# Weight sums by accumulating transfers, one more block by seven products, and a new order for the second token group

## The chip, the cores and the metric

The kernel runs on one core of one Trainium2 chip. The metric is the device time of one execution in microseconds; the median of several executions is compared.

## The reference, cut to what matters

The program is a chunked state-space scan followed by a two-layer network with a sigmoid-weighted activation.

```
y = mamba2_ssd(x, a, B, C)            # 4 sequences, 8 heads, 768 steps, head size 32, state 16
h = y @ w_in                          # 3072 tokens x 256, w_in 256 x 2048
g = h * (1.0 / (1.0 + np.exp(-1.702 * h)))
out = g @ w_out                       # w_out 2048 x 256
```

The weights arrive as 64-bit floats and are rounded to 32 bits in the kernel.

## The kernel before, in words

The 3072 tokens are worked in six groups of 512 (`g` = 0 to 5), each of two pairs of chunks (`p`, `p + 1`). For each pair the scan part makes a decay table (`decay`, a VectorE scan into `L`, line 424, and two products into `Be`, line 489), scores (`score`, TensorE, line 682, masked inputs from `mask_blocks`, ScalarE, line 659), their weighting (`weigh`, VectorE, line 693), the state increments (`gain`, TensorE, line 713), the states (`keep_both`: ScalarE line 767 or VectorE line 769, then steps on VectorE, line 782), and the outputs (`finish`: `inter`, line 822, and `intra`, line 836, on TensorE, and copies into `yT` on ScalarE, lines 869 and 871). The scan part of group g + 1 is put between the products of group g.

The network has eight blocks `j` per group, each of 256 hidden units. There are two ways to work a block of the first layer. `hidden` (line 896) is the plain one: four matmuls of 128x128 by 512 columns for the block's two halves. `first` (lines 952 and 962) works the block as a 2x2 by 2x2 product with seven products of 256 columns instead of eight (Winograd's form). Its steps are named by digits: "1", "6", "7", "4" build up in one PSUM bank X and are copied out in between by ScalarE (line 957); "5", "2", "3" build up in a second bank Y. "D" adds (VectorE, line 1084), "S" and "T" activate (ScalarE, line 929). The second layer has the same two ways: `project_all` (line 994) plain, `product` (line 1057, in the last group line 1064) with seven products per block into one large PSUM area, combined at the group's end by `combine` (line 1088).

Seven products need sums of the weight quarters and of the data quarters. `mix_in(n)` makes four sums of `w_in` for blocks 2n and 2n + 1, `mix_w(n)` the same of `w_out`; each is four VectorE operations of 128x256 (lines 914 and 1017). `mix_y` and `mix_g` make the sums of the data, three VectorE operations each (lines 920 to 922). All weight sums are made once and used from group 1 on. Group 0 is plain throughout; in group 1 blocks 0 and 1 of the first layer are plain, all else is by seven products.

The order of work is written by hand: `in_order` keeps every engine in the order of the program text. During group 0's second layer, the table `in_project[0]` places other work ahead of a given `f`; `after` does so behind group 1's two pairs of plain calls; from then on a string such as "2.1 3.1 2.5" gives the order of steps, in which a digit pair is a block and its step, "P" is the next second-layer product, and a letter runs a given function. `steady(j)` and `closing(k)` are the repeated strings. VectorE, ScalarE and POOL work ahead of TensorE as far as their data allow.

Transfers are issued by SP's queue, in program order: tables `ra` (line 275), blocks of B and C (line 124), and `b`, `c`, `x` (line 150). `x` has three buffers: the `x` of a pair is loaded once the one three pairs earlier is read. POOL has little to do after 13 us: for each `clip_rows` a memset (line 511), a copy (line 513) and a small memset (line 514), which `decay_rows` (line 522) waits for.

SBUF tiles with one tag share a few buffers. `words` (tag "bits", four buffers of 2048 words a partition) holds the raw weights and later `ra` and the sums of `w_out`; "m" and "p2" (two each of 1024 words) hold parts of the raw weights and later the sums of `w_in`. In PSUM, the "ff" tag has four banks for X, Y, `hidden` and `gain`, and the "cb" area of four banks holds in turn the scores, the outputs of `finish` and the sums of the second layer.

Of the kernel before, what the change touches and what calls it, by code (L numbers as in the profile page):

```python
# [8 lines left out]
FP32 = mybir.dt.float32  # L9
# [6 lines left out]
GELU_SCALE = 1.702  # L16
# [19 lines left out]
def kernel(  # L36
# [224 lines left out]
    scratch = dram.tile([NC, 2, NB * NH, H], FP32, name="scratch")  # L261
    ra = {}

    def spread(p, held=False):

        if p - 2 in ra:
            ra[p] = ra[p - 2]
        else:
            ra[p] = words(f"a{p}").bitcast(FP32)[:, :2 * NH * H].rearrange(
                "p (k e) -> p k e", k=2)  # L270
        if held:
            nc.vector.memset(ra[p][:, 0, :1], 0.0)
        b, c = divmod(2 * p, NC)
        for i, side in enumerate(SIDES):
            nc.sync.dma_start(
                out=ra[p][side],
                in_=scratch[c:c + 2, i, b * NH:(b + 1) * NH].rearrange("c h i -> c (h i)").unsqueeze(
                    0).to_broadcast([H, 2, NH * H]))
# [625 lines left out]

    def mix_in(n):

        t = wide.tile([P, PN], FP32, tag=("m", "p2")[n % 2], name=f"mi{n}").rearrange(
            "p (j s e) -> p j s e", j=2, s=4)
        w = w_in[:, 4 * n:4 * (n + 1)].rearrange("p (j i) k e -> p j i k e", i=2)
        a11, a12, a21, a22 = w[:, :, 0, 0], w[:, :, 0, 1], w[:, :, 1, 0], w[:, :, 1, 1]  # L910
        s1, s2, s3, s4 = (t[:, :, i] for i in range(4))
        for o, u, v, op in ((s1, a21, a22, ALU.add), (s2, s1, a11, ALU.subtract),
                            (s3, a11, a21, ALU.subtract), (s4, a12, s2, ALU.subtract)):
            nc.vector.tensor_tensor(out=o, in0=u, in1=v, op=op)
        for k in range(2):
            mixed_in[2 * n + k] = t[:, k]

    def mix(t, B):

        nc.vector.tensor_tensor(out=t[:, 0:2], in0=B[:, :, 1], in1=B[:, 0], op=ALU.subtract)  # L920
        nc.vector.tensor_tensor(out=t[:, 2], in0=B[:, 1, 1], in1=t[:, 0], op=ALU.subtract)
        nc.vector.tensor_tensor(out=t[:, 3], in0=B[:, 1, 0], in1=t[:, 2], op=ALU.subtract)

# [3 lines left out]

    def silu(o, i):
        nc.scalar.activation(o, i, AF.Silu, scale=GELU_SCALE)  # L929

    def first(g, j, i):
# [4 lines left out]
        B = yT[g].rearrange("p k (t e) -> p k t e", t=2)  # L936
        T, S = mixed_y[g], mixed_in[j]
        A = w_in[:, 2 * j:2 * j + 2].rearrange("p i k e -> p k i e")
# [8 lines left out]
        if i in "1674":  # L947
            lhsT, rhs, copy = {"1": (A[:, 0, 0], B[:, 0, 0], s["ac"][:, 0]),
                               "6": (S[:, 1], T[:, 2], s["b"]),
                               "7": (S[:, 2], T[:, 1], s["ac"][:, 1]),  # L950
                               "4": (A[:, 1, 1], T[:, 3], None)}[i]
            nc.tensor.matmul(out=s["X"], lhsT=lhsT, rhs=rhs, start=i == "1", stop=i == "4",  # L952
                             skip_group_check=True)
            if copy is None:
                silu(gT[g, j][:, 1, :HT], s["X"])
            else:
                nc.scalar.activation(copy, s["X"], AF.Copy)  # L957
        elif i in "523":
            lhsT, rhs, o = {"5": (S[:, 0], T[:, 0], s["Y"][:, 1]),
                            "2": (A[:, 1, 0], B[:, 1, 0], s["Y"][:, 0]),  # L960
                            "3": (S[:, 3], B[:, 1, 1], s["Y"][:, 1])}[i]
            nc.tensor.matmul(out=o, lhsT=lhsT, rhs=rhs, start=s.pop("new", False), stop=i != "5",  # L962
                             skip_group_check=True)
            if i == "3":
                plus(gT[g, j][:, 0, HT:], s["Y"][:, 1], s["b"])
        elif i == "T":
            c12 = gT[g, j][:, 0, HT:]
            silu(c12, c12)
        else:
            if i == "D":  # L970
                block(g, j)
            c = gT[g, j].rearrange("p i (t e) -> p (i t) e", t=2)[:, 0:4:3]
            if i == "D":
                plus(c, s["Y"], s["ac"])
            else:
                silu(c, c)

# [9 lines left out]
    def project_all(g, between):  # L987

        o = [bank(f"o{g}_{c}") for c in range(2)]
        for f in range(NF):  # L990
            for do in between.get(f, []):
                do()
            for c in range(2):
                nc.tensor.matmul(out=o[c], lhsT=w_out[:, c, f],  # L994
                                 rhs=gT[g, f // 2][:, f % 2], start=(f == 0),
                                 stop=(f == NF - 1), skip_group_check=True)
        sums[g] = ffn.tile([P, 2, 2, HT], FP32, tag="gT", name=f"c{g}", bufs=6)
        for c in range(2):
# [6 lines left out]

    def mix_w(n):

        if n % 2 == 0:
            mixed_w["tile"] = words(f"mw{n}").bitcast(FP32).rearrange(
                "p (n j s e) -> p n j s e", n=2, j=2, s=4)  # L1010
        t = mixed_w["tile"][:, n % 2]
        w = w_out[:, :, 4 * n:4 * n + 4].rearrange("p c (j i) e -> p c j i e", i=2)
        a11, a12, a21, a22 = w[:, 0, :, 0], w[:, 0, :, 1], w[:, 1, :, 0], w[:, 1, :, 1]
        s1, s2, s3, s4 = (t[:, :, i] for i in range(4))
        for o, u, v, op in ((s1, a21, a22, ALU.add), (s2, s1, a11, ALU.subtract),
                            (s3, a11, a21, ALU.subtract), (s4, a12, s2, ALU.subtract)):
            nc.vector.tensor_tensor(out=o, in0=u, in1=v, op=op)
        for k in range(2):
            mixed_w[2 * n + k] = t[:, k]

# [7 lines left out]
    def product(g, j, only=ORDER, ks=range(2)):  # L1028
        if j == 0 and g not in acc:
# [3 lines left out]
            else:  # L1033
# [11 lines left out]

        terms = ((A[:, 0, 0], B[:, 0, 0]), (A[:, 0, 1], B[:, 1, 0]), (S[:, 1], T[:, 2]),
                 (S[:, 0], T[:, 0]), (S[:, 2], T[:, 1]), (S[:, 3], B[:, 1, 1]),
                 (A[:, 1, 1], T[:, 3]))
# [45 lines left out]
    def combine(g):  # L1094
# [5 lines left out]
        scaled(u[:, 1:3], a[:, 3:5], u[:, 2:3].to_broadcast([P, 2, HT]))  # L1100
        scaled(c[:, 1, 0], a[:, 6], u[:, 2])
        scaled(c[:, 0], a[:, 1:6:4], u[:, 0:2])
        sums[g] = c
        rest = lambda: plus(c[:, 1, 1], u[:, 2], u[:, 3])
        if g < NG - 2:
# [18 lines left out]
    def end(g, j0):  # L1124
# [21 lines left out]
        scaled(u2, p7, u2)  # L1146
        plus(c[:, 1, 1], u2, u5)
        put(1, nc.scalar)
        products(1)
        scaled(c[:, 1, 0], p4, u2)  # L1150
        scaled(c[:, 0, 0], p2, u1)
# [88 lines left out]
    for i, k, c in ((2, 1, 1), (3, 2, 3), (4, 4, 7), (5, 8, 10), (6, 10, 14), (7, 14, 15)):  # L1240
# [15 lines left out]
    at(in_project[0], 15, lambda: finish(pairs))  # L1256
    at(in_project[0], 13, lambda: mix_in(1), lambda: turn_blocks(2), lambda: decay(n))
    at(in_project[0], 6, lambda: spread(n), lambda: spread(n + 1), lambda: load_blocks(n),
# [6 lines left out]
    later = n, n + 1  # L1265
    at(after, "H0", lambda: decay(n + 1), lambda: mix_y(1), lambda: since_start(n),
       lambda: since_start(n + 1), lambda: gain(later), lambda: keep_both(later, True), lambda: score(later),
       lambda: weigh(n), lambda: weigh(n + 1))
    at(after, "H1", lambda: turn_out(0, 0), lambda: turn_out(0, 1), lambda: mix_in(2),
       lambda: mix_w(0))  # L1270
    assert [b for b in range(NB) if 3 * CG <= b * NC < 4 * CG] == [2]

# [5 lines left out]
    project_all(0, in_project[0])  # L1278
    mask_blocks(n)
    mask_blocks(n + 1)  # L1280
    load_blocks(p)
    spread_rows(2)
    load(p, "bx")
    for step in "H0", "H1":
        for i in range(2):
            hidden(1, 2 * int(step[1:]) + i)
        for do in after[step]:
            do()

# [37 lines left out]
    def more_loads():  # L1327
# [3 lines left out]

    run(1, "2.1 3.1 2.5 2.6 3.6 z 2.2 2.7 3.5 3.7 3.2 2.D 2.4 3.D 3.4 2.S W 3.S y m 2.3 3.3 4.1 2.T 3.T",
        m=lambda: mix_g(1, 0),
        z=lambda: finish(later, (0,)), y=lambda: finish(later, (1,)), W=lambda: clip_rows(2))
    mix_g(1, 1)
    more_loads()
    mix_in(3)
    decay_rows(2)
    run(1, "4.5 4.2 P P 4.6 P P 4.7 P P P 4.D", seven(1, 0))
    mix_w(1)  # L1340
    mix_g(1, 2)
    decay(p)
    between = {5: (lambda: mix_g(1, 3), lambda: mix_w(2)),
               6: (lambda: mix_g(1, 4), lambda: decay(p + 1)),
               7: (lambda: mix_g(1, 5), lambda: mix_w(3))}
    for j in range(5, NF // 2):
        run(1, steady(j), seven(1, j - 4), M=lambda: [do() for do in between[j]])
    k = NF // 2 - 1
    run(1, closing(k), seven(1, 4))
    mix_g(1, 6)  # L1350
    mix_in(0)
    run(1, "P P A P P P P P", seven(1, 5), A=lambda: ahead(2, p))
    mix_g(1, 7)

    for g in range(2, NG):
# [28 lines left out]
        def refill():  # L1384
            if most:
# [4 lines left out]
                spread(p + 1)  # L1390

        if more:

            run(g, "2.1 1.S 1.4 1.3 2.6 2.5 2.2 2.7 1.T 3.1 s 2.D 2.S w 2.4 2.3 3.6 M0 3.5 3.2 3.7 2.T 4.1 y "
                "refill 3.D 4.5 4.2 4.6 3.4 3.3 P P P 3.S P 3.T M1 4.7 P P P 4.D M2",
                seven(g, 0), s=lambda: score((n, n + 1)), w=lambda: (weigh(n), weigh(n + 1)),
                y=lambda: finish((n, n + 1)), refill=refill,
                M0=lambda: mix_g(g, 0), M1=lambda: mix_g(g, 1), M2=lambda: mix_g(g, 2))
# [61 lines left out]
```

## Time and profile before

| | |
|---|---|
| runs | 345.81, 345.05, 346.56 us; median 345.81 |
| the profiled execution | 345.17 us, of which its span 343.4 us |
| TensorE matmul busy | 338.3 us (98%) |
| VectorE busy | 255.5 us (74%), 486 instructions |
| ScalarE busy | 155.8 us (45%) |
| POOL busy | 13.3 us (4%), 40 instructions |
| transfers | 25.75 MB, mean 75 GB/s; SP's queue 34.8% of 16 engines' span |
| granted TensorE clock | 1.00 |

Group 0's first layer runs from 17.6 to 45.2 us, its second layer from 45.6 to 78.2, group 1 from there to about 131 us. Busy times of engines are not shares of the path: the chain of work that ended last says what set the end.

### The profile page before, as it was taken

What the parts mean: (1) busy time and instruction counts of PE and PEld (TensorE: products, weight loads), DVE (VectorE), ACT (ScalarE), POOL (GpSimd) and SP (SyncE); (2) the same over time, 40 slices, a digit from 0 to 9 for tenths busy, and PEclk for the clock granted to TensorE, in tenths of its full rate; (3) what the DMA queues carried; (4) which work ended last, traced back from release to release, by engine and by line L of the source; (5) the groups of instructions that cost most, each with busy time, mean ns of one, the idle gap of its engine ahead of it and who ended that gap; (6) DMA issues with size and microseconds to landing.
All of it is one profiled execution on the core that took longest, in us unless ns stands there. A gap on an engine that the chain in (4) does not pass through costs nothing.

```text
span 343.4 us, 8128 instructions
## 1 busy us (share of the span) xinstructions
PE 338.3 (98%) x3378; PEld 271.2 (79%) x3378; DVE 255.5 (74%) x486; ACT 155.8 (45%) x356; POOL 13.3 (4%) x40
## 2 busy tenths in 40 slices
PE   8999999999999999999999999999999999999996
PEld 6645744555788888888888888888888888899996
DVE  6989999999999797858995667787564653465463
ACT  5798672406563314554333554342553422554320
POOL 6100010200010000000000000000000000000000
DMA  6699978455737000345513036400000300000402
GB/s 166 138 296 210 323 158 151 107 84 106 116 80 123 7 2 22 56 111 92 108 32 46 2 86 115 63 3 0 2 3 2 61 2 0 0 2 0 63 0 62
DMA packets 90020, 25.75 MB, mean 75 GB/s; under 512 B 73440, under 2 KB 87264, under 8 KB 89984
## 3 DMA queue, kind: packets, MB, share of 16 engines
q1 hardware_dynamic: 89152, 24.72, 34.8%
q8 instruction: 26, 0.43, 0.6%
q10 hardware_dynamic: 832, 0.52, 0.5%
q14 instruction: 10, 0.08, 0.1%
HBM read 21.99 MB, written 3.24 MB: 73 GB/s over the span
## 4 chain that ended last, share of the span: by engine, by line
PE 97%; DMA 1%; ACT 0%; DVE 0%; issue 0%; ACTq 0%; DVEq 0%
PE acc L1057 28%; PE X L952 19%; PE Y L962 15%; PE h L896 10%; PE o L994 8%; PE acc L1064 7%; PE y L836 3%; PE cb L682 2%; PE y L822 1%; PE A L713 1%; PE ab L556 1%; DMA az<-in_a_dram 1%; PE tp L599 0%; DVE cum L359 0%; ACT yT L856 0%
## 5 line engine op out<-in xcount | busy, mean ns | idle before, releaser
L957 ACT ACTIVATE ac<-X 128x256 f32<-128x256 f32 x76 | 29.0, 382 | 83.9 <-PE X L952 83.8
L1057 PE MATMUL acc<-mg,mw 128*128 128x256 f32 x192 | 53.9, 379 | 0.0
L1084 DVE TENSOR_TENSOR gT<-Y,ac 128x512 f32<-128x512 f32 x38 | 26.2, 689 | 37.0 <-PE Y L962 34.5
L929 ACT ACTIVATE gT<-gT 128x512 f32<-128x512 f32 (+1 forms) x76 | 38.9, 519 | 26.1 <-DVE gT L1084 25.5
L952 PE MATMUL X<-my,mi 128*128 128x256 f32 x152 | 45.1, 379 | 0.0
L1057 PEld LDWEIGHTS acc<-mg,mw 128*128 128x128 f32 x192 | 36.5, 190 | 4.9
L1084 DVE TENSOR_TENSOR gT<-Y,b 128x256 f32<-128x256 f32 x38 | 16.0, 420 | 28.7 <-PE Y L962 28.7
L896 PE MATMUL h<-yT,w_in 128*128 128x512 f32 (+1 forms) x96 | 35.1, 524 | 0.5 <-ACT yT L856 0.5
L1057 PE MATMUL acc<-gT,w_out 128*128 128x256 f32 x128 | 35.5, 379 | 0.0
L952 PEld LDWEIGHTS X<-my,mi 128*128 128x128 f32 x152 | 28.2, 190 | 3.6
L896 PEld LDWEIGHTS h<-yT,w_in 128*128 128x128 f32 x96 | 18.1, 190 | 16.0 <-issue 12.4
L994 PE MATMUL o<-gT,w_out 128*128 128x512 f32 x64 | 28.3, 596 | 0.0
L920 DVE TENSOR_TENSOR mg<-gT 128x512 f32<-128x512 f32 x40 | 27.3, 681 | 0.0
L1057 PEld LDWEIGHTS acc<-gT,w_out 128*128 128x128 f32 x128 | 24.4, 190 | 3.3
L957 ACT ACTIVATE b<-X 128x256 f32<-128x256 f32 x38 | 14.6, 383 | 19.2 <-PE X L952 18.5
L962 PE MATMUL Y<-my,mi 128*128 128x256 f32 x76 | 23.0, 384 | 0.0
L952 PE MATMUL X<-my,w_in 128*128 128x256 f32 x76 | 22.8, 384 | 0.0
L962 PE MATMUL Y<-yT,w_in 128*128 128x256 f32 x76 | 22.7, 381 | 0.0
L962 PE MATMUL Y<-yT,mi 128*128 128x256 f32 x76 | 22.6, 381 | 0.0
L994 PEld LDWEIGHTS o<-gT,w_out 128*128 128x128 f32 x64 | 11.9, 190 | 13.6 <-issue 13.1
L952 PE MATMUL X<-yT,w_in 128*128 128x256 f32 x76 | 22.5, 379 | 0.0
L424 DVE TENSOR_TENSOR_SCAN L<-a,idents 128x1024 f32<-128x1024 f32 x9 | 20.5, 2279 | 0.0
(152 smaller groups left out, 546.2 us busy)
## 6 DMA issues: line engine op xcount, KB each, us to landing
a<-scratch SPq DMA_DIRECT2D x18, 256.0 KB, 4.6
bits<-in_moe_w_out_dram SPq DMA_DIRECT2D x8, 512.0 KB, 8.4
x<-in_x_dram SPq DMA_DIRECT2D x24, 128.0 KB, 3.7
out_dram<-ob SPq DMA_DIRECT2D x37, 64.0 KB, 2.0
bits<-in_moe_w_in_dram SPq DMA_DIRECT2D x8, 256.0 KB, 4.8
bits<-in_moe_w_in_dram SPq DMA_DIRECT2D x4, 512.0 KB, 8.9
b<-in_B_dram SPq DMA_DIRECT2D x20, 64.0 KB, 3.5
af<-in_a_dram SPq DMA_DIRECT2D x3, 384.0 KB
```

The lines of the kernel that those rows point to most:

```text
L424: nc.vector.tensor_tensor_scan(out=L, data0=ra[p].rearrange("p k e -> p (k e)"), data1=idents.rearrange("p h i -> p (h i)"), initial=0.0, ...
L836: nc.tensor.matmul(out=y[i][t][D * q:D * q + D, 2 * n + k], lhsT=rx[p][side, k, h], rhs=L[side, k, h // Q, h % Q], start=begin(i, t, (q,)) ...
L896: nc.tensor.matmul(out=h[:, cols], lhsT=w_in[:, f, k], rhs=yT[g][:, k, cols], start=(k == 0 and c == 0), stop=(k == NK - 1), skip_group_ch ...
L920: nc.vector.tensor_tensor(out=t[:, 0:2], in0=B[:, :, 1], in1=B[:, 0], op=ALU.subtract)
L929: nc.scalar.activation(o, i, AF.Silu, scale=GELU_SCALE)
L952: nc.tensor.matmul(out=s["X"], lhsT=lhsT, rhs=rhs, start=i == "1", stop=i == "4", skip_group_check=True)
L957: nc.scalar.activation(copy, s["X"], AF.Copy)
L962: nc.tensor.matmul(out=o, lhsT=lhsT, rhs=rhs, start=s.pop("new", False), stop=i != "5", skip_group_check=True)
L994: nc.tensor.matmul(out=o[c], lhsT=w_out[:, c, f], rhs=gT[g, f // 2][:, f % 2], start=(f == 0), stop=(f == NF - 1), skip_group_check=True)
L1057: nc.tensor.matmul(out=acc[g][0][i][:, cols], lhsT=w, rhs=h[:, cols], start=(j == 0 and k == 0 and (i, 0) in begins), stop=(j == NF // 2 - ...
L1064: nc.tensor.matmul(out=o[k] if type(o) is list else o[:, cols], lhsT=h[:, cols], rhs=w, start=(j == 0 and (i, k) in begins), stop=(j == NF ...
L1084: nc.vector.tensor_tensor(out=o, in0=v, in1=w, op=ALU.add)
```

## The change

Three things are changed together.

**Who makes the weight sums.** `sums_of` makes the four sums of a tile in four steps, by transfers that POOL's queue issues: step 0 copies one weight quarter into the first half and others into the second, step 1 adds the remaining weights to the first half, steps 2 and 3 add parts of the tile to each other. An added transfer has `accum_op=ALU.add`. Only additions are left, so signs go elsewhere: `mix` takes differences the other way round with `minus_both` (a scalar_tensor_tensor for a tensor_tensor), "4" and one half of "S" activate with the scale -1.702, so that "S" is two activations of 256 columns for one of 512, and the combination at the end of a group subtracts. `mix_in(2)`, `mix_in(3)` and all of `w_out`'s sums (now two calls of `mix_w`, each for four blocks) go this way, from group 0's second layer on. `mix_in(0)` and `mix_in(1)` stay on VectorE (`js=`), the first in two parts, one per block.

**Block 1 of group 1** goes by seven products for two plain `hidden` calls; block 0 stays plain.

**Group 1 in a new order.** `mix_in(1)`, `turn_blocks(2)` and `decay(n)` leave the table `in_project[0]` at 13, and with the rest of `after` they go into one string that begins with "M1 1.1 B h Q D4 K Y E i M0 A c s k". `decay_rows(2)` goes from ahead of block 4 into block 6's steady string. The two `turn_out(0, ...)` with their stores go to group 2; until then group 0's output lies in the unused half of a `ra` tile (`spare`).

```diff
-    ra = {}
+    ra, spare = {}, []
...
+            t = words(f"a{p}").bitcast(FP32)
+            ra[p] = t[:, :2 * NH * H].rearrange("p (k e) -> p k e", k=2)
+            spare.append(t[:, 2 * NH * H:])
...
+    SLOTS = {"3": (0, 0), "1": (0, 1), "2": (1, 0), "4": (1, 1)}
+
+    def sums_of(tiles, n, js, new, first, w, step):
+        if n not in tiles:
+            tiles[n] = new().rearrange("p (h j s e) -> p h j s e", h=2, j=js, s=2)
+        one, two = tiles[n][:, 0], tiles[n][:, 1]
+        def put(o, i, **how):
+            nc.gpsimd.dma_start(out=o, in_=i, **how)
+        if step == 0:
+            first(one)
+            put(two, w(0))
+        elif step == 1:
+            put(one, w(1), accum_op=ALU.add)
+        elif step == 2:
+            put(two[:, :, 0], one[:, :, 1], accum_op=ALU.add)
+        elif step == 3:
+            put(two[:, :, 1], two[:, :, 0], accum_op=ALU.add)
...
+    def mix_in(n, steps=range(4), js=None):
...
+        if js:
...
+            plus(one[:, :, 0], a[:, :, 0, 0], a[:, :, 1, 0])
+            plus(one[:, :, 1], a[:, :, 1, 0], a[:, :, 1, 1])
+            plus(two[:, :, 0], one[:, :, 1], a[:, :, 0, 0])
+            plus(two[:, :, 1], two[:, :, 0], a[:, :, 0, 1])
+            return
+        for step in steps:
...
+                lambda o: nc.gpsimd.dma_start(out=o.rearrange("p j s e -> p (j s) e"), in_=w[:, :, 0]),
...
     def mix(t, B):
-        nc.vector.tensor_tensor(out=t[:, 0:2], in0=B[:, :, 1], in1=B[:, 0], op=ALU.subtract)
-        nc.vector.tensor_tensor(out=t[:, 2], in0=B[:, 1, 1], in1=t[:, 0], op=ALU.subtract)
-        nc.vector.tensor_tensor(out=t[:, 3], in0=B[:, 1, 0], in1=t[:, 2], op=ALU.subtract)
+        nc.vector.tensor_tensor(
+            out=t[:, 0:2], in0=B.rearrange("p k t e -> p (k t) e")[:, 0:4:3],
+            in1=B[:, 0, 1:2].to_broadcast([P, 2, HT]), op=ALU.subtract)
+        minus_both(t[:, 2], t[:, 0], B[:, 1, 1])
+        minus_both(t[:, 3], t[:, 2], B[:, 1, 0])
...
-                silu(c, c)
+                for k in range(2):
+                    silu(c[:, k], c[:, k], 1 - 2 * k)
...
-        sums[g] = ffn.tile([P, 2, 2, HT], FP32, tag="gT", name=f"c{g}", bufs=6)
+        sums[g] = spare[-1].rearrange("p (c t e) -> p c t e", c=2, t=2)
...
-    at(in_project[0], 13, lambda: mix_in(1), lambda: turn_blocks(2), lambda: decay(n))
+    for k in range(4):
+        at(in_project[0], 7 + k, lambda k=k: mix_w(0, (k,)), lambda k=k: mix_in(2, (k,)))
+    for k in range(4):
+        at(in_project[0], 14, lambda k=k: mix_in(3, (k,)), lambda k=k: mix_w(1, (k,)))
...
-    run(1, "2.1 3.1 2.5 2.6 3.6 z 2.2 2.7 3.5 3.7 3.2 2.D 2.4 3.D 3.4 2.S W 3.S y m 2.3 3.3 4.1 2.T 3.T",
...
-    run(1, "4.5 4.2 P P 4.6 P P 4.7 P P P 4.D", seven(1, 0))
+    run(1, "M1 1.1 B h Q D4 K Y E i M0 A c s k 2.1 v 2.5 2.2 1.6 2.6 w 1.5 1.7 2.7 2.D 1.2 1.4 z 3.1 1.D 2.3 1.S 2.T G 1.3 2.S 3.6 3.2 y 3.7 C 4.1 3.5 3.D 2.4 1.T L P P H 4.6 P P P P 4.5 4.2 3.3 4.7 P 4.D 3.T I 3.S 3.4 N", seven(1, 0),
```

In the new string the letters stand for: M1 `mix_in(1)`, B `turn_blocks(2)`, h and i the two `hidden` calls of block 0, Q and K `mask_blocks` of the second and the first pair, D4 and E `decay` of the two pairs, Y `mix_y(1)`, M0 block 1's half of `mix_in(0)`, A `gain`, c `score`, s `since_start`, k `keep_both`, v and w `weigh` of the second and the first pair, z and y the two halves of `finish`, G, H and I `mix_g`, C `clip_rows(2)`, L loads for group 3, N `decay` for it.

## The prediction

> **What bounds the kernel now.** I read the page's first and fourth parts, then TensorE's own waits, then the table of engines by stretches of 10 us.
>
> ```profile
> PE 338.3 (98%) x3378; PEld 271.2 (79%) x3378; DVE 255.5 (74%) x486; ACT 155.8 (45%) x356; POOL 13.3 (4%) x40
> ...
> PE 97%; DMA 1%; ACT 0%; DVE 0%; issue 0%; ACTq 0%; DVEq 0%
> ```
>
> ```profile
> PE busy L468 <- DVE ones L313: 1.1, 1, 1.1
> PE h L896 <- ACT yT L856: 0.5, 1, 0.5
> PE ab L556 <- DVE cum L359: 0.3, 1, 0.3
> PE y L836 <- issue: 0.2, 1, 0.2
> PE b L629 <- ACT L L577: 0.2, 1, 0.2
> ```
>
> TensorE ends the chain and waits five times, 2.3 us in all, always before 17.58 us, which the change doesn't touch. Busy time of pipelined matmuls can hide gaps, so I also took the distances between matmul starts. From 17.58 to 340.7 us each record follows the last by its own width, 0.43 us for 512 columns and 0.216 for 256. The exceptions are 0.09 to 0.19 us where a run of small matmuls (lines 682, 713, 822, 836) begins or ends. So only less TensorE work can shorten the middle, and any new wait there lengthens the run one for one.
>
> ```profile
> 60.00:70.00 10.00, 10.00 (x139) 4.95 (x138) 9.61 (x15) 3.77 (x13) 2.56 (x3) 1.00 0.39 100
> 70.00:80.00 10.00, 10.00 (x203) 5.48 (x202) 9.93 (x12) 3.27 (x7) 0.00 (x0) 1.00 0.69 101
> 80.00:90.00 10.00, 10.00 (x195) 6.01 (x198) 9.16 (x22) 5.95 (x18) 0.00 (x0) 1.00 0.57 109
> 90.00:100.00 10.00, 10.00 (x196) 8.62 (x190) 9.42 (x23) 5.75 (x14) 0.66 (x2) 1.00 0.38 60
> ```
>
> Columns after the stretch: sum of time, then busy time of PE, PEld, DVE, ACT, POOL, then the granted clock (1.00), the DMA share and GB/s. Around the end of group 0 (78 us) VectorE has 9.2 to 9.9 us of work in 10: it is nearly late here, and here the order changes.
>
> **TensorE's part.** Each product shows as two records. Block 1 of group 1 costs two `hidden` calls now: eight records of 512 columns.
>
> ```profile
> 81.71 0.87 PE L713 MATMUL A<-x,Be 64*32 64x64 f32 x56
> 82.51 1.21 PE L682 MATMUL cb<-CT,Bt 32*64 32x128 f32 x64
> 83.65 3.70 PE L896 MATMUL h<-yT,w_in 128*128 128x512 f32 x8
> 87.19 1.03 PE L952 MATMUL X<-yT,w_in 128*128 128x256 f32 x4
> ```
>
> From 83.65 to 87.19 less one change of form (0.10) is 3.44 us. Seven products are 14 records of 0.216, 3.02 us. **Saved: 0.42 us.** Nothing else on TensorE changes in number.
>
> **VectorE's part.** Gone from group 1 are six calls of `mix_in`/`mix_w`, 24 additions of 128x256 at 0.42 us (lines 914, 1017): 10.1 us. Two transposes of line 1114 (1.3 us) go to group 2, where VectorE is 7.3 us busy in 10. `mix_in(0)` becomes eight additions of 128x128, at 0.28 each (row of line 769) 2.2 us for 1.7. `mix` swaps two tensor_tensor of 128x256 (425 ns) for scalar_tensor_tensor (424 ns, line 1088): nothing. None of this is on the path by itself, since TensorE waits for nothing.
>
> **ScalarE's part.** "S" becomes two activations of 128x256 (413 ns) for one of 128x512 (625): +0.2 us, 39 times, 7.8 us in all on an engine that is 45% busy. `mix_g`, which reads the result, stands about a block later in the steady order; before the last block's there is about 1 us to spare (first sum done at 332.5, wanted near 333.5). I cost it at nothing; without that cover it would be 0.2 us at that place.
>
> **The new start of group 1.** I put the operations in program order on three lines, with the durations above, from TensorE's 78.18 us. VectorE's order up to there is the same: four sums, two transposes, `decay(4)` to 78.0. Then `mix_y` comes first (1.5, to 79.6), `decay(5)` (2.7, to 82.3) and block 1's sums (1.1, to 83.4). TensorE does 1.1, h, i (0.43 + 1.72 + 1.72) to 82.05. `gain`, with its first half (0.5) on pair 4, wants pair 5 at about 82.5: just met, where 1 us was spare before. Two places are late:
>
> - "z" wants both `weigh` calls, because its area is theirs. VectorE reaches their end by 83.4 + 0.75 (`since_start`) + 2.6 (eight steps of line 782) + 2.26 = 89.0. TensorE is there at 82.05 + `gain` 1.0 + `score` 1.34 + ten products 4.3 + 0.1 = 88.8. **Wait 0.24 us** with the hand-over.
> - the first P wants the area that "y" held, so ScalarE's three copies (1.8, lines 869 and 871). Five products stood between before, four now (1.83 us with the change of form, against 1.99): **wait 0.16 us**.
>
> Hidden calls and gains get their PSUM banks in time: `gain`'s second bank follows h's activation at 81.0, block 2's Y follows `gain`'s copies at about 84.6.
>
> **The transfers.** 22 go on POOL's queue: five for each of two `mix_in` (1.0 MB written), six for each of two `mix_w` (2.0 MB), in four steps that each wait for the landing of the one before. No transfer from POOL and no accumulating one is in this trace. POOL is free at 61.9, after the copy and memset of `clip_rows(1)`. Group 1 first reads these sums in product 4.6, at about 97 us: 35 us for the first eleven. Behind the chain on POOL stands only `clip_rows(2)`; `decay_rows(2)`, which waits for it, is moved to block 6, near 110. From below: moving 512 bytes took one DMA engine 27 ns, so the 3.0 MB of the first chain is 10 us on 16 engines. From above: a 256 KB load from memory took 4.6 us to land, and twelve of those end to end are 55 us. I take the four steps at up to 8.5 us (the row of the 512 KB loads), 34 us at worst and nearer 22 with small later steps: ready at 84 to 96, hidden.
>
> [...]
>
> **Sum.** -0.42 + 0.24 + 0.16 = -0.02 us. The profiled execution took 345.17 us (span 343.4, 1.8 around it); the three runs 345.05 to 346.56, median 345.81. The mean of these four is 345.65, so I predict **345.6 us**: the change gives TensorE 0.4 us and takes about as much back in waits. About 0.5%, 1.7 us, is what a measurement of this kernel can tell from no change.
>
> **The rivals.**
>
> 1. *Slower: the x of pair 5 lands late.* The DMA engines are full where the new chain runs.
>
> ```profile
> 72.19 2.43 SPq L150 DMA_DIRECT2D b<-in_B_dram  x4
> 74.67 3.85 SPq L150 DMA_DIRECT2D x<-in_x_dram  x4
> ```
>
> From 73 to 80.1 us the packets of b and x fill 6.3 of 7.1 us of all 16 engines, and the last x packet ends at 80.1. `gain` wants it at 82.5. If POOL's transfers take every second turn, 6.3 us become up to 12.6 and the last x ends at 86.5: 4 us late. It decides from 2.4 us of transfer time put in between. Half of that chain would be over by 73, so some 1 to 2 us late is the middle of this case: 347.5, at most 349.7. Chance 0.10.
>
> 2. *Slower: POOL is held up by VectorE, and the sums are late for 4.6.*
>
> ```profile
> 59.42 2.29 DVE L424 TENSOR_TENSOR_SCAN L<-a,idents 128x1024 f32<-128x1024 f32 x1
> ```
>
> ```profile
> 59.63 2.08 POOL L513 COPY first<-af 128x12 f32<-128x12 f32 x1 [14.57 <-DVE af L508]
> 94.09 0.54 POOL L513 COPY first<-af 128x12 f32<-128x12 f32 x1 [25.86 <-DVE af L508]
> ```
>
> The same copy took 1.54 us longer beside a scan and ended with it. If each of eleven transfers loses that, 17 us come on top of 22: ready at 101, 4 us late, 349.6. It decides at 35 us for the chain. Chance 0.07.
>
> [...]
>
> 3. *No waits appear.* The estimates of 0.24 and 0.16 are near the error of the hand-over times. Then -0.42: 345.2. It lies within the forecast's side of "same"; with the forecast 0.79.
>
> 4. *Faster by over 1.7 us.* VectorE's 10 us would have to be on the path, against the dense starts: 0.04.
>
> All 0.79 of forecast and rival 3 fall within 0.5%; the rivals that reach beyond it on the slow side hold 0.17. Range: from rival 3 with the lowest run, 345.05 - 0.42 = 344.6, up to rival 1's middle, 347.8. It leaves out the far parts of rivals 1, 2 and 4.
>
> **What would show it.** Right: 14 records where eight of 512 columns stood; TensorE's waits in group 1 below 0.5 us in all, at lines 822 and 1057; sums landed before 96 us; VectorE below 9 us in 10 between 90 and 120. Wrong: a wait at line 713 on x (rival 1); a wait of several us at the first product that reads transferred sums (rival 2); a VectorE operation longer than its row while POOL issues, which nothing in this trace shows.

## The result, and the profile after

The changed kernel takes **364.77 us** (median of four runs, 363.62 to 366.36); the kernel before, run beside it, 346.19 us (345.05 to 347.14). The ratio is 1.054 (1.049 to 1.060): 18.6 us slower, above the predicted range. The profiled execution took 363.62 us, its span 361.6 us. In the runs below, one execution of `v1` took 895.57 us and one of `v2` 501.38; the ratios leave them out, and nothing is read from `v1`'s trace, which is of the first.

The page of the changed kernel first: busy times, the granted clock in 40 slices of 9 us, POOL's new queue (packets, MB, share of 16 engines' span), and the chain that ended last.

```profile
PE 344.3 (95%) x3384; PEld 275.4 (76%) x3384; DVE 249.5 (69%) x468; ACT 159.3 (44%) x399; POOL 34.5 (10%) x62
...
PEclk9999999998799999999989999999999999999999
...
q0 software_dynamic: 4960, 6.29, 9.0%
...
PE 92%; DMA 3%; issue 2%; SPq 1%; DVE 1%; ACT 0%; POOL 0%; POOLq 0%; DVEq 0%
```

TensorE has six records more, as forecast (14 for 8). Yet its busy time grew by 6 us: the clock row has two dents, in which matmuls ran slowly for 4.2 us in all (below). And transfers and "issue" now hold 5% of a chain that was 97% TensorE's. TensorE's waits:

```profile
PE A L714 <- DMA x<-in_x_dram: 5.1, 3, 2.8
PE X L991 <- ACT ac L998: 4.3, 1, 4.3
PE y L837 <- issue: 1.8, 2, 1.2
```

The distances between matmul starts show where the 18.1 us of span went:

| place in the changed kernel | us |
|---|---|
| `gain` waits for the x of pair 5, 82.6 to 89.0 us | +5.5 |
| matmuls at a clock of 0.50 right behind it, to 94.6 us | +2.5 |
| a stop with nothing to wait for, in `intra` at 102 us | +1.45 |
| a wait at 178 us, in group 2 | +4.45 |
| a clock of 0.50 behind that, 183 to 187 us | +1.7 |
| a stop at 272 us | +0.45 |
| start, up to group 0's first product (18.60 for 17.58; 17.2 to 18.2 in the other kernels) | +1.0 |
| end, from the last matmul on (3.9 for 3.0) | +0.85 |
| block 1 by seven products | -0.43 |

These sum to 17.5 us; the rest is spread over gaps of under 0.3 us. (The expectations below put the two low-clock rows at 3.2 and 1.4 us. Set against the same matmuls in `v4`, at a clock of 1.00, the slow ones lose 2.5 and 1.7.)

**The first wait** is read from four views. The stretches (sum, busy PE, PEld, DVE, ACT, POOL, granted clock, DMA share, GB/s) stand against those of before:

```profile
70.00:80.00 10.00, 10.00 (x203) 5.57 (x202) 5.60 (x10) 2.24 (x5) 3.33 (x3) 1.00 1.03 223
80.00:90.00 10.00, 4.89 (x72) 2.18 (x78) 9.38 (x16) 2.95 (x8) 7.37 (x9) 0.90 1.35 175
90.00:100.00 10.00, 10.00 (x155) 8.27 (x155) 5.88 (x13) 4.66 (x17) 3.05 (x3) 0.76 1.08 256
```

The DMA share was 0.69, 0.57 and 0.38 there; now the packets' times add up to more than the 16 engines' time. SP's queue in the same time (start, length, line):

```profile
73.88 2.59 SPq L124 DMA_DIRECT2D zB<-in_B_dram  x4
76.51 5.10 SPq L150 DMA_DIRECT2D b<-in_B_dram  x4
81.66 3.67 SPq L150 DMA_DIRECT2D x<-in_x_dram  x4
```

x is issued at 81.66 us, 7.0 us later than before, and its last part lands at 88.9. (1.0 us of this is the later start of the whole trace, in the table above.) Only part of the delay is x's own: the blocks of C and B ahead of it land late, SP's own waits, from 60 to 90 us, name their landing four times, 2.4 us in all, and the b loads spread over 5.1 us for 2.4. VectorE is late by the same cause:

```profile
78.59 1.11 DVE L638 STREAM_TRANSPOSE Ct<-zC 128x512 f32<-128x512 f32 x1 [3.96 <-DMA zC<-in_C_dram]
...
87.88 0.49 DVE L490 TENSOR_TENSOR Be<-b,L 128x128 f32<-128x128 f32 x2
```

It waits 4.0 us for a block of C, and the `Be` of pair 5, which `gain` also needs, ends at 88.4. Had x alone been on time, `gain` would still have waited until then. The low clock shows in TensorE's own rows:

```profile
89.00 0.94 PE L714 MATMUL A<-x,Be 64*32 64x64 f32 x24 [1.70 <-DMA x<-in_x_dram]
89.88 2.01 PE L683 MATMUL cb<-CT,Bt 32*64 32x128 f32 x64
91.82 1.22 PE L991 MATMUL X<-yT,w_in 128*128 128x256 f32 x2
```

The 64 score products took 1.21 us before and take 2.01 here; matmuls of 256 columns start 0.43 us apart until 94.6 us, then 0.216 again.

**The second wait** is named after ScalarE, but the row of that engine ends long before. Going back from it, VectorE's transpose for the output waits for a store, and SP's queue shows why:

```profile
178.33 0.71 DVE L1156 STREAM_TRANSPOSE ob<-c 128x512 f32<-128x512 f32 x1 [5.63 <-DMA out_dram<-ob]
```

```profile
171.83 12.86 SPq L1164 DMA_DIRECT2D out_dram<-ob  x16
```

Group 0's two output transposes, now in group 2, fill both `ob` tiles at 159.6 us. Their stores stand on SP behind the loads of `refill` and are issued from 171.8 on. VectorE's next transpose, of group 1's output, needs one of those tiles; the adds for TensorE's next blocks are queued behind it.

### The profile page after: what moved, and what is told of

Its sections match the earlier page's. It is cut to its first block, busy times and chain, and to the rows that moved or that the text cites. A ratio compares the mean times of both kernels' runs of the same rounds, so it can differ in the third digit from the quotient of the medians.

```text
span 361.6 us, 8210 instructions
## 1 busy us (share of the span) xinstructions
PE 344.3 (95%) x3384; PEld 275.4 (76%) x3384; DVE 249.5 (69%) x468; ACT 159.3 (44%) x399; POOL 34.5 (10%) x62
## 4 chain that ended last, share of the span: by engine, by line
PE 92%; DMA 3%; issue 2%; SPq 1%; DVE 1%; ACT 0%; POOL 0%; POOLq 0%; DVEq 0%
PE acc L1099 26%; PE X L991 19%; PE Y L1003 14%; PE o L1036 8%; PE h L897 8%; PE acc L1106 7%; PE y L837 3%; PE cb L683 2%; DMA x<-in_x_dram 1%; PE A L714 1%; PE y L823 1%; DMA out_dram<-ob 1%; SPq L150 1%; PE busy L469 1%; PE ab L557 1%
## 5 line engine op out<-in xcount | busy, mean ns | idle before, releaser
L967 ACT ACTIVATE gT<-gT 128x256 f32<-128x256 f32 x117 | 43.4, 410 | 30.5 <-DVE gT L1126 30.0
L991 PE MATMUL X<-my,mi 128*128 128x256 f32 x156 | 47.1, 385 | 4.6 <-ACT ac L998 4.3
L991 PEld LDWEIGHTS X<-my,mi 128*128 128x128 f32 x156 | 29.3, 193 | 9.3 <-ACT ac L998 4.7
L959 DVE SCALAR_TENSOR_TENSOR mg<-mg,gT 128x256 f32<-128x256 f32 x80 | 34.0, 425 | 2.8
L897 PE MATMUL h<-yT,w_in 128*128 128x512 f32 (+1 forms) x88 | 31.4, 516 | 0.5 <-ACT yT L857 0.5
L897 PEld LDWEIGHTS h<-yT,w_in 128*128 128x128 f32 x88 | 16.6, 190 | 14.0 <-issue 10.8
L1003 PE MATMUL Y<-my,mi 128*128 128x256 f32 x78 | 24.1, 391 | 0.0
L991 PE MATMUL X<-yT,w_in 128*128 128x256 f32 x78 | 23.9, 389 | 0.0
L1003 PE MATMUL Y<-yT,w_in 128*128 128x256 f32 x78 | 23.7, 386 | 0.0
L1003 PE MATMUL Y<-yT,mi 128*128 128x256 f32 x78 | 23.5, 386 | 0.0
```

The costliest lines, as they stand in the source:

```text
L897: nc.tensor.matmul(out=h[:, cols], lhsT=w_in[:, f, k], rhs=yT[g][:, k, cols], start=(k == 0 and c == 0), stop=(k == NK - 1), skip_group_ch ...
L959: nc.vector.scalar_tensor_tensor(out=o, in0=v, scalar=-scale, in1=w, op0=ALU.mult, op1=ALU.subtract)
L967: nc.scalar.activation(o, i, AF.Silu, scale=sign * GELU_SCALE)
```

## The experiments

Each ratio is against the kernel before, run beside it (medians 345.81, 345.23, 345.62 and 345.54 us).

### The late stores: `u1_stores_early`

```diff
-               7: (lambda: mix_g(1, 5),)}
+               7: (lambda: mix_g(1, 5), lambda: turn_out(0, 0), lambda: turn_out(0, 1))}
...
-            if g == 2:
-                for i in range(2):
-                    turn_out(0, i)
```

> The changed kernel, with group 0's two output transposes and their sixteen stores put behind block 7's step of group 1, where SP's queue is idle, and no longer in group 2. Theory (two separate losses, traffic around 82 us and late stores around 178 us): TensorE's wait of 4.45 us at 178 us and the 1.4 us of slow clock behind it go, 364.8 - 5.9 = 358.9 us; the wait for x at 82 us stays. Rival (the wait at 178 comes from VectorE having too much to do there, not from the stores' buffer): VectorE gets only 1.3 us less in group 2, so 363.5 us or more.

Measured: 357.47 us, ratio 1.031 (1.026 to 1.036). The wait at 178 us is gone, the one for x stays:

```profile
PE A L714 <- DMA x<-in_x_dram: 5.2, 4, 3.1
```

The place of two transposes and their stores cost 7.3 us by the medians, 5.8 by the spans.

### The transfers: `u2_vector_sums`

The string and block 1 as in the changed kernel, the late stores too; all sums by VectorE, four additions of 128x256 each, at n2, w0, w1 and n3 in the string and at two blocks' ends.

```diff
...
-    for k in range(4):
-        at(in_project[0], 7 + k, lambda k=k: mix_w(0, (k,)), lambda k=k: mix_in(2, (k,)))
-    for k in range(4):
-        at(in_project[0], 14, lambda k=k: mix_in(3, (k,)), lambda k=k: mix_w(1, (k,)))
...
```

> The changed kernel with all weight sums made by VectorE and no transfer from POOL; the new order, block 1 by seven products and the late stores stay. Theory (the 6.3 MB of POOL's transfers delay SP's loads, and that makes TensorE wait for x): the wait for x (5.5 us), the slow clock behind it (3.2) and the 1.4 us stop at line 837 go, about 364.8 - 10 = 354.7 us, with x landed near 81 us again. Rival (the new order is late by itself, because VectorE reaches the pair's decay too late): TensorE still waits several us at line 714, 360 us or more.

Measured: 354.67 us, ratio 1.025 (1.021 to 1.029).

```profile
80.00:90.00 10.00, 9.80 (x193) 6.82 (x195) 9.46 (x21) 6.56 (x20) 0.00 (x0) 1.00 0.43 86
90.00:100.00 10.00, 10.00 (x194) 8.21 (x192) 8.33 (x20) 5.59 (x15) 0.40 (x2) 1.00 0.19 35
```

TensorE is full and the clock 1.00 where the changed kernel lost 8 us; x waits for 0.2 us. The stores still cost 4.3 us at 170 us. Putting all sums into the string made VectorE late once, 1.2 us at 110 us.

### The order: `u3_transfers_old_order`

The transfers alone, with the old order of group 1, block 1 plain and the stores in group 1.

> The transfers alone: sums by POOL's transfers as in the changed kernel, but the old order of group 1, block 1 plain, group 0's stores in group 1. Theory (traffic): x lands near 88 us here too, gain waits for it some 6 us, a slow clock costs some 3 us more, about 346.2 + 10 = 356 us, and there is no wait at 178 us. Rival (the order is to blame): 346 to 348 us.

Measured: 357.88 us, ratio 1.036 (1.030 to 1.042): as slow as `u1`, with the same wait for x (5.5 us). The profiled execution, the longest of the four (361.35 us), has a second wait of 4.7 us at 117 us, where the decay of pair 6 waited 7 us for a load of SP's; that load stood behind group 0's eight stores, which took SP 8.3 us for 5.3 before. The traffic does the harm in either order, and the rival falls.

### The clock: `u4_filled`

```diff
+    def fill():
+        t = area("fill")[:, 0]
+        for _ in range(13):
+            dense(4, t)
...
-        A=lambda: gain(later), ...
+        A=lambda: [fill(), gain(later)], ...
```

> The changed kernel with thirteen extra matmuls of 128x128 by 256 columns of ones (5.6 us of work that nothing reads) ahead of gain, where TensorE waits for x. Theory (the clock falls because TensorE was idle): the clock stays at 1.00 from 80 to 100 us, the wait is covered by the extra work, and the 3.2 us of slow matmuls go: about 361.5 us. Rival (the clock falls for another reason, such as the traffic): still slow matmuls there, 364.8 us or more.

Measured: 363.38 us, ratio 1.048 (1.043 to 1.053), less than hoped.

```profile
80.00:90.00 10.00, 9.81 (x142) 7.21 (x148) 9.33 (x17) 3.34 (x10) 7.16 (x8) 1.00 1.43 191
90.00:100.00 10.00, 8.98 (x186) 7.20 (x172) 7.56 (x16) 5.52 (x19) 3.31 (x3) 1.00 1.09 243
```

The DMA engines are as full as in the changed kernel, and the clock stays at 1.00: in the changed kernel TensorE's idleness lowered it (to 0.90 and 0.76 in these stretches), not the traffic. In the profiled execution (363.46 us) other losses grew and took the gain back: stops without a wait, at 99 and 267 us, cost 1.9 and 2.0 us (1.45 and 0.45 in the changed kernel), and the clock fell to 0.50 behind the second, from 271.1 to 274.5 us, for another 1.5. The DMA share there is 0.02, so that dip too came without traffic. One of the four executions took 360.73 us, at a mean clock of 1.00.

### No transfers, early stores: `w1_vector_early`, `v1_vector_filled`, `v4_vector_spread`

`w1` is `u2` with the early stores and its sums spread over group 1.

> New order and seven products for block 1, but no transfers at all: VectorE makes every weight sum (as in the run with VectorE's sums), the stores of the first two output blocks go back into group 1, and the sums and decay tables stand where VectorE is not late for the product at 111 us. From that run's 354.67 us the stores' wait (4.28 us and about 1.4 us of low clock behind it) and the wait of 1.2 us at 111 us should go: 347.8 us. The theory that transfers and stores are the whole loss expects 346 to 349, granted clock 1.00 from 20 us on, and no wait over 0.5 us. The rival, that the new order itself costs something that the other waits covered, expects 350 or more, with waits in group 1.

Measured: 347.46 us, ratio 1.0057 (1.0037 to 1.0076), clock 1.00. One wait of 0.79 us before group 2's first product, at 129 us, stands against the theory's last clause: VectorE had next to no idle time from 103 us on. In `v1` one group of sums moves from 103 to 99 us (w1 ahead of L in the string).

> As the run with VectorE's sums and early stores (347.46 us), with one group of sums (two blocks of the second layer's) moved from about 103 us to about 99 us, where VectorE was idle 1.3 us for want of a product. That run waited 0.79 us at 129 us because VectorE had no idle time from 104 us on. If that is all of it, the wait goes and the time is 346.5 to 347.0: then the new order and the seven products, without transfers and late stores, cost what the prediction's sum said, nothing that can be measured, and the rest of the 2 us lies outside group 1. If the order has another cost that moves along, 347.3 or more, with another wait in group 1.

Measured: 347.52 us, ratio 1.0048 (1.0030 to 1.0065). Nothing is gained. `v2` below, with the same string but for n2, shows why: VectorE is idle for 2.0 us at 107 us and then not at all until 132; the work that was moved lay ahead of the idle stretch, not in the full one behind it. `v4` moves the scan of `decay_rows(2)` out of the full stretch:

```diff
-3.S 3.4 n3"
+3.S 3.4 n3 R"
...
+        R=lambda: decay_rows(2), ...
```

> As the run without transfers and with one group of sums moved (347.5 us, whose wait at about 130 us stayed), with the scan for token block 2 (1.75 us on VectorE) moved from about 112 us, where VectorE has no idle time until 132 us, to about 106 us, where it has 2.0 us. Theory: the wait of 0.8 us before group 2's first product goes, and the time is 346.5 to 347.0; what is then left over the kernel before is the wait at z, the stops at 258 us and the 0.8 us longer end. Rival: the wait comes from something else (the products' results, say) and stays: 347.3 to 347.7.

Measured: 346.97 us, ratio 1.0036 (1.0021 to 1.0051). Only one wait is left in the whole middle that the wait view names:

```profile
PE b L630 <- ACT L L578: 0.2, 1, 0.2
PE y L823 <- DVE L L694: 0.2, 1, 0.2
```

(The first is at the start.) From group 0's first product to the last matmul it takes 323.29 us, 0.47 more than before: 0.43 saved, 0.28 lost at z, 0.24 at the first P, 0.4 in three more places. The end adds 0.88. Together 1.35 of the 1.43 us between the medians. (The two profiled executions lie 0.5 us further apart, by their starts: 18.07 for 17.58.) This is the change without its two expensive parts, and it is no faster than the kernel before, by the interval 0.2 to 0.5% slower; nor is any other version here faster.

### Accumulation or bytes: `w3_copies`

```diff
-            put(one, w(1), accum_op=ALU.add)
+            put(one, w(1))
```

and the same for steps 2 and 3, with the early stores of `u1`.

> The changed kernel with the early stores (357.47 us), in which the accumulating transfers are plain copies of the same bytes from the same places; the weight sums are thereby replaced by copies of single weights, so the output is not the reference's. Theory A, the bytes and packets of POOL's queue crowd the other loads whatever is done with them: the wait for x at gain stays within 1 us of 5.2 and the time at 356 to 358.5. Theory B, accumulation makes each packet dear (65 ns where 27 ns stood for 512 bytes): packets of POOL's queue fall below 45 ns, x lands some 3 us earlier, and the time is 353 to 354.5.

Measured: 356.3 us, ratio 1.031 (1.028 to 1.034), a wait for x of 5.4 us: theory A. This kernel leaves the additions out. One part of B held all the same, that POOL's packets take less time in all:

```profile
q0 software_dynamic: 1888, 6.29, 6.1%
```

The same bytes took 9.3% of the engines' span in `u1`, with accumulation, and 6.1% without. The packets differ in size too, 512 and 1024 bytes for the accumulating transfers and 4096 for the plain ones, so the cost of the addition itself isn't separated. The saving did not reach `gain`. SP issued x 1.25 us earlier than in `u1` (79.93 us for 81.18), but POOL, done sooner with the first chain, also issued the second chain's copies sooner, at 82.1 us for 85.1, beside the packets of x. The last matmuls of `gain` started at 90.2 us, for 88.7 in `u1`.

### Later instead of fewer: `w4_held`, `w2_held_half`

```diff
+    hold = const.tile([P, 1], FP32, name="hold")
+    at(in_project[0], 14, lambda: nc.gpsimd.tensor_copy(hold, rx[n + 1][:, 1, 0, :1]))
...
-        at(in_project[0], 7 + k, lambda k=k: mix_w(0, (k,)), lambda k=k: mix_in(2, (k,)))
+        at(in_project[0], 14, lambda k=k: mix_w(0, (k,)), lambda k=k: mix_in(2, (k,)))
```

> The changed kernel with the early stores (357.47 us), all of its transfers held until the x of pair 5 has landed (a copy on POOL reads that x first). Theory: x is there at about 80 us, the wait at gain and the low clock behind it go (about 8 us back), but the first chain of four steps, which took 24 us, now ends near 105 us where product 4.6 wants its sums near 97 us: a wait of some 8 us there and again a low clock behind it, so 355 to 358. Rival: with the loads out of the way the chain is shorter, 14 to 16 us, and the wait there is below 1 us: 348 to 350.

Measured: 368.32 us, ratio 1.065 (1.061 to 1.069), slower than the changed kernel. x was in time, and a wait of some 8 us came as the theory said, but both expected times were missed: the chain took 29 us (82.6 to 111.9), although SP's loads for pair 5 were out of its way, and TensorE stood still for 7.9 and 3.2 us. A third stop of 2.6 us came at 133 us, and the clock stood at 0.50 for 13.7 us behind the first two and for 3.4 behind the third.

```profile
100.00:110.00 10.00, 1.19 (x2) 0.50 (x2) 0.41 (x1) 0.38 (x1) 5.66 (x8) 0.64 1.15 168
```

The longer wait is listed as "issue", without a releaser. POOL's queue names it: the third step of the sums for blocks 4 and 5 was issued at 100.9 us, its last packet ended at 105.8, and TensorE went on at 106.4. So the chain as it is fits neither ahead of x, where it makes x late, nor behind it, where its last packet ends 13 us after TensorE first stopped for it. `w2` keeps only the second chain, held in the same way, on top of `w1`.

> Like the run before it in this call, but the sums for blocks 6 and 7 of the first layer and 4 to 7 of the second are made by POOL's accumulating transfers, which begin only when the x of pair 5 has landed (a copy on POOL reads it first). Half the transferred bytes, moved behind the loads that they held up. Theory (the time of the transfers, not their kind, did the harm): x lands before 81 us, no wait at gain, the chain takes about 22 us from 81 and ends by 105, ahead of its first use near 109 us: 346 to 347, less than 1 us from the run without transfers. Rival (accumulating transfers harm whatever stands beside them, TensorE's clock or later loads too): 350 or more, with waits for loads of x, B or C after 85 us.

Measured: 348.87 us, ratio 1.0108 (1.0073 to 1.0143). The chain took 30 us (81.4 to 111.1) where 22 were expected, but no sum was late, and x by no more than 0.3 us. What cost 1.4 us over `w1` was neither theory:

```profile
PE y L837 <- issue: 2.4, 1, 2.4
```

a stop inside `intra`, of which more at the end.

### The dose: `v2_third_early`, `v3_two_thirds_early`

`v1` with a part of the first chain back at its place, 1.05 and 2.10 MB.

> As the first run of this call, with a third of the first chain's transfers put back where the changed kernel has them (the sums for two blocks of the first layer, 5 transfers from about 62 us on). By the packets of the changed kernel they are some 5 us of all engines' time, half of it ahead of the x of pair 5. Theory (the wait for x grows with the transfer time put in ahead of it): a wait at gain of 0 to 2 us, 346.7 to 349.5. Rival (any chain on POOL's queue holds up SP's loads by itself): a wait of 4 us and more with a low clock behind it, 352 or more.

> As the run before it, but with the other two thirds of the first chain (6 transfers, the second layer's sums for four blocks, from about 62 us on): some 10 us of all engines' time. Theory: a wait at gain of 2 to 4.5 us, between that of the run before it and the 5.2 us of the full traffic, with a part of the low clock behind it: 349.5 to 353.5. Rival (it is the number of chains or of steps, not the bytes): as the run before it, within 1 us.

Measured: 349.45 us, ratio 1.0103 (1.0077 to 1.0129), and 352.3 us, ratio 1.0194 (1.0142 to 1.0245). In `v2` `gain` stopped once for 1.1 us; in `v3` three times, 1.9 us in all, and the clock fell to 0.83 in 80 to 90 us. With none, a third, two thirds and all of the first chain ahead of x (`u1`, which also has the second behind it), the times are 347.5, 349.5, 352.3 and 357.5: the loss grows with the bytes. (`v3`'s four times spread from 349.98 to 354.89; what VectorE sums differs from version to version as well.) In `v2` the larger part of the stop is VectorE's:

```profile
PE A L714 <- DVE Be L490: 0.9, 1, 0.9
...
PE A L714 <- DMA x<-in_x_dram: 0.4, 2, 0.2
```

## Why the prediction was wrong

The step that failed is "ready at 84 to 96, hidden", the end of the paragraph on the transfers. The time of the sums was nearly right: the first chain ran from 63.4 us to 89.5, where its last packet ended, 26 us for an estimate of 22, and no product ever waited for a sum in the changed kernel. But "hidden" was judged only by when the sums are needed, not by what the transfers do to others.

That effect was rival 1, the wait at line 713 (now 714) on x, with a chance of 0.10 and at most 4 us. It was the main case, and its size was off in three ways, all shown above.

- I had stretched only b's and x's own packets, by a factor of two. The whole row of loads ahead of them was stretched too, so x began 7.0 us late (1.0 of it by the later start); it landed at 88.9, not 86.5. That half of the chain "would be over by 73" failed as well: its first step alone took until 71 to 75 us.
- VectorE's chain to `Be` hung on the same loads of C and B, and was as late as x. I had costed `decay(5)` at 82.3 us; it ended at 88.4.
- Behind the wait of 5.5 us the clock was 0.50: 2.5 us that stood in no sum. `u4` shows that idleness did it.

With the stop at 102 us these are 9.5 us; the medians of `u1` and of `v1` and `v4` differ by 10 to 10.5.

The second failure is one clause: "Two transposes of line 1114 (1.3 us) go to group 2, where VectorE is 7.3 us busy in 10". The step was moved, but of what it issues I counted only the transposes. Their stores were moved past `refill`'s loads on SP, and `ob` has two buffers. `u1` puts this at 5.8 to 7.3 us.

What was right: 0.42 us saved (0.43); the wait at z, 0.24 (0.20 by the wait view, 0.28 by the starts); the wait at the first P, 0.16 (0.24); `gain` just met without transfers (x waited for 0.2 us in `u2`). So the sum of -0.02 us described a kernel without the transfers and the late stores, `v4`, within 1.4 us. Of that difference 0.88 us is the longer end. Rival 2 did not show: POOL's issues took 0.6 to 1.3 us, and POOL waited for landings, not for VectorE. ScalarE's two activations for one cost 3.5 us in all instead of 7.8, off the path: two of 256 columns in a row take 0.71 us together, since they overlap, where one of 512 took 0.625. "Faster" had nothing behind it: VectorE's 6 us less are in no path. The range's upper end, 347.8, is called rival 1's middle, which was worked out as 347.5; neither comes near.

## What to carry to other kernels

A transfer that is ready in time isn't therefore free (here no product waited for a sum, and the transfers cost some 9.5 us): list every load in flight beside it, and follow each one's delay through its queue and its tile's buffers to the engine that waits. When a step moves, its stores move too (here 5.8 to 7.3 us); ask what stands ahead of them on the queue and who needs their buffer next. In the changed kernel the waits of 5.5 and 4.45 us on a dense TensorE cost 2.5 and 1.7 us more than themselves, by the stretches at a clock of 0.50 behind them.

## What the runs showed of the hardware that I had not expected

- **Instruction packets among the transfers.** The trace has 26 packets of 16 KB in a queue of the kind "instruction" (0.43 MB, 0.5% of the 16 engines' span in the changed kernel). In the kernels with the new order but `u4`, wherever TensorE stopped in `intra` of group 1 for "issue", it stopped at the same place, behind the 1231st matmul of the trace, and such a packet had just begun: 0.01 us ahead of that matmul in `w2` (next matmul 2.57 us later), 0.6 in `u1` (1.71), 0.9 in the changed kernel (1.45), 1.5 in `w4` (1.27), 1.8 in `v2` (0.4). Where it had begun 2.4 us ahead or more (`u2`, `w1`, `v4`, `w3`, `v3`) the next matmul followed within 0.2 us. In all ten the next matmul started 2.2 to 3.1 us after the packet. `u4` has 26 matmuls more ahead of that place; its two stops in `intra` lie behind the 1231st and the 2883rd matmul (as the changed kernel's stops at 102 and 272 us do), with 3.0 and 2.6 us from the packet's start to the next matmul. So it is the count of matmuls that recurs, not the step of the program. In `w2` the packet began 96 matmuls later in the program than in `w1`, which differs by the transfers; the DMA share over 90 to 100 us was 1.01 in `w2` and 0.07 in `w1`, and that full engines delayed the packet is my guess, not tried by itself.
- **The longer end.** In every kernel with the new order whose trace is read, the last matmul starts 3.7 to 4.4 us before the end, in the kernel before and `u3` 3.0 to 3.1. In all of these an 8 KB instruction packet runs within the last 2.6 us, and the last eight 512-byte packets of the last store follow 0.3 to 0.4 us after the others; before and in `u3` none is there. Whether it is the cause stays open.
- **The clock after a wait.** In the changed kernel the waits of 5.5 and 4.45 us were followed by a granted clock of 0.50, from 87.9 to 94.7 us and from 183.5 to 186.9. With shorter stops it could go either way. A stop of 2.57 us in `w2` had no slow stretch behind it; one of 1.97 us in `u4`, at 267.7 us, had (the clock was 0.50 from 271.1 to 274.5). In `v3` three stops of 0.3, 0.8 and 0.9 us within 2.8 us were enough (0.83 over 80 to 90 us). In every trace with such stretches the changes of the clock lie a whole multiple of 3.41 us apart (in the changed kernel 6.83, 88.75 and 3.41 us), so it may matter where in such a step a stop falls; that was not tried.
- **Accumulating packets** of 512 bytes took 65 ns on POOL's queue (median, changed kernel); plain ones on SP's took 27. Plain packets of 4096 bytes took 211 in `w3`, the same time per byte as the 27 (0.05 ns).
